# Moving two groups of an expert's rows into a scheduled list, and giving routing rows a buffer each

## The chip, the cores and the metric

The kernel runs on one core of one Trainium2 chip. The metric is the device time of one execution in microseconds (us), the median of the runs shown. A core has TensorE (PE, matrix products), VectorE (DVE), ScalarE (ACT) and GpSimd (POOL) for the work, and SyncE (SP), which here issues nearly all DMA transfers. Each engine takes its instructions in the order in which the program gives them to it.

## What is computed

Three layers follow each other: a gated delta attention, a mixture of experts in which every token goes through all 8 experts (weights from 8 Sinkhorn rounds), and a second mixture in which each token goes to its one best expert.

```
# attention, per batch and head, 768 steps, head_dim 48
y[t]  = q[t] @ state
state = state + beta[t] * outer(k_n[t], v[t] - k_n[t] @ state)
# first mixture: x is (3072, 384), w1 (8, 384, 1024), w2 (8, 1024, 384)
P = exp(x @ w_gate - max);  8 times: P /= P.sum(1); P /= P.sum(0); P *= N / E
out = sum over e of P[:, e] * (relu(x @ w1[e]) @ w2[e])
# second mixture: cosine logits / tau, argmax, one expert per token
out[mask_e] = gate_w[mask_e] * (relu(x[mask_e] @ w1[e]) @ w2[e])
```

## The kernel before

Tokens lie in 24 tiles of 128, which make 6 groups of 512. Matrix products run in float16 with a high and a low half for each operand, so each product is three matmuls.

**The attention's list.** The attention, the whole of expert 0, and the first half of expert 1's hidden units (4 of 8 blocks of 128) are nodes of a list. A small planner, class `Sched`, walks through the nodes with a table of costs (`HOP` from one engine to another, a cost for each node, and a choice of engines where a node has several) and so sets the order in which each engine gets its instructions; it runs while the program is built. The expert nodes (line 824 for the first layer, 848 for the second) fill TensorE between attention nodes. Their results for each tile are copied by ScalarE (858) and stored by SyncE to DRAM: `y0d` for expert 0, `y1d` for expert 1's first half (859). The Sinkhorn rounds are nodes of the same list. At its end stand the first layer of group 0 of expert 1's second half (1050) and the second layer of tile 0 (1063). In the list a second-layer result `py` has one PSUM buffer (pool `ps2`).

**Behind the list** everything is written in loops. SyncE loads the accumulator `accb` (24 tiles, 4.7 MB) from `y0d` in six transfers (1197). `moe1_group(1, W, g)` loads the group's four tiles of `y1d` (374), runs the first layer (352, with ScalarE 335 and VectorE 336 splitting each block of 512 into halves), and then, tile by tile, the second layer (363); for expert 1 each tile then gets ScalarE's scaling of `accb` by expert 0's weight (383), VectorE's adding of the `y1d` half (384) and of `py` (387). Here `py` has two buffers (`ps3`), as has the first layer's `pt`. Between the steps `run` calls `bg()`, every third step, which puts a piece of the next expert's weight preparation into the program (`prep_w`: load into `st` 286 and 288, six maxima 295, a maximum over partitions by GpSimd 302, six splits by ScalarE 274 and VectorE 275, and so twice for each expert).

**The routing.** Expert 7 of the first mixture and the routing of the second are a second list. For each group of four tiles the best expert and a place in a table are worked out; `row` (token number and weight) is written by GpSimd into the table with four indirect transfers (1446), at the places in `ri`. `row` has two buffers, so the copy that begins the row of group g (1420) waits until the transfers of group g - 2 have landed.

Of the kernel before, what the change touches and what calls it, by code (L numbers as in the profile page):

```python
# [165 lines left out]
def kernel(  # L166
# [202 lines left out]
    def moe1_group(e, W, g):  # L369

        fs, x = (FH, "b") if e == 1 else (0, e)
        if e == 1:
            yh_ = st2.tile([128, 4, DM], F32, name="yh", tag="yh", bufs=2)
            nc.sync.dma_start(out=yh_, in_=y1d[4 * g:4 * g + 4].rearrange("t p d -> p t d"))
        if (e, g) != (1, 0):
            yield from mlp1(W, xh[g], xl[g], 512, hh, hl, fs)
# [41 lines left out]
    with (  # L418
# [623 lines left out]
        o1 = {}  # L1042
        pn = None
        for f_ in range(FH):
            for kk in range(KD):
                def f(slot=None, f_=f_, kk=kk):
                    if kk == 0:
                        o1[f_] = ps1.tile([128, 512], F32, name="pt")
                    for x, (wv, xv) in enumerate(((0, xh), (0, xl), (1, xh))):
                        nc.tensor.matmul(out=o1[f_], lhsT=w1v(W1, wv, kk, FH + f_), rhs=xv[0][:, kk], start=kk == 0 and x == 0, stop=kk == KD - 1 and x == 2)  # L1050
                Q((f"h{f_}_{kk}", "e1"), "P", 648, f, [pn] if pn else [("xb", 0), mend] + w1a, 2e6,
                  ps=("pt", 1) if kk == 0 else None, cols=1536, moe=True)
                pn = (f"h{f_}_{kk}", "e1")
            wr = [mend]
            Q((f"rl{f_}", "e1"), "A", 478, lambda f_=f_: nc.scalar.activation(out=hh[f_], in_=o1[f_], func=AF.Relu), [pn] + wr, NT - 1.0)
            Q((f"rs{f_}", "e1"), "V", 602, lambda f_=f_: nc.vector.scalar_tensor_tensor(
                out=hl[f_], in0=o1[f_], scalar=0.0, in1=hh[f_], op0=ALU.max, op1=ALU.subtract), [(f"rl{f_}", "e1")], NT - 1.0, frees=(f"h{f_}_0", "e1"))
        for f_ in range(FH):
            def f(slot=None, f_=f_):
                if f_ == 0:  # L1060
                    pye.append(ps2.tile([128, 512], F32, name="py"))
                for x, (a_, b_) in enumerate(((hh, 0), (hh, 1), (hl, 0))):
                    nc.tensor.matmul(out=pye[0][:, 0:DM], lhsT=a_[f_][:, 0:128], rhs=w2v(W1, b_, FH + f_),
                                     start=(f_ == 0 and x == 0), stop=(f_ == FH - 1 and x == 2))
            Q((f"g{f_}", "e1"), "P", 488, f, [pn, (f"rs{f_}", "e1")] + w1, 2e6, ps=("py", 1) if f_ == 0 else None, cols=1152, moe=True)
            pn = (f"g{f_}", "e1")
# [231 lines left out]
    def route_tile(g, j):  # L1298
# [72 lines left out]
    def route_group(g):  # L1371
# [350 lines left out]
```

## Time and profile before

| | us |
|---|---|
| median of 3 runs | 2196.34 (2196.14 to 2198.1) |
| the profiled execution, its own time | 2194.12 |
| its span, first to last instruction | 2192.3 |
| PE busy | 2046.6 (93%) |
| DVE busy | 1227.4 (56%) |
| ACT busy | 849.9 (39%) |

The profile gives for each engine the time in which it works, and for its idle time what ended it. TensorE is busy nearly all the time, so what counts is where it isn't, and what it waits for there. Matmuls overlap in its pipeline; the distance of the starts tells the true cost. The list of the attention ends for TensorE at about 702 us, expert 1 at 798 us, expert 6 at about 1738 us; the second mixture begins at about 1960 us.

### The profile page before, as it was taken

Reading aid. Unit: us, or ns where it says so; the run is one execution under the profiler, and the core shown is the slowest. Engines: PE = TensorE matmul, PEld = TensorE weight load, DVE = VectorE, ACT = ScalarE, POOL = GpSimd, SP = SyncE. Lnnn points to the kernel's source line nnn. Section 1 sums busy time; section 2 is a strip of 40 time slices with the busy share of each in tenths; the row PEclk is TensorE's granted clock in tenths of the full one; section 3 lists DMA queues with packets and bytes.
Section 4 is the critical chain, followed back from the end, with each engine's and each line's share of the span. In section 5 each row is a group of like instructions: output and inputs, shape, how many; then the busy total and the mean of one; then the engine's idle time right before and its main releaser. Section 6 shows DMA issues by size and latency. Waiting matters only on the chain. (4 is left out here: it accounts for less than half of the span.)

```text
span 2192.3 us, 46083 instructions
## 1 busy us (share of the span) xinstructions
PE 2046.6 (93%) x19340; PEld 1293.5 (59%) x19340; DVE 1227.4 (56%) x2815; ACT 849.9 (39%) x1600; POOL 277.3 (13%) x322
## 2 busy tenths in 40 slices
PE   2688999999998999999999999999999989999999
PEld 2667777777765445555555555555555545557777
DVE  7988888888771665445445545554552245552111
ACT  5766756566532332223222322222221134352332
POOL 5322323233100000000000000000000000112221
PEclk9799999999999999999999999999999999999999
DMA  2546666566534220231132123113220001049765
GB/s 88 111 98 117 130 118 113 106 124 119 129 97 148 71 85 29 87 114 59 58 116 87 59 87 107 67 58 116 76 69 1 1 19 26 19 136 345 273 238 204
DMA packets 367237, 224.90 MB, mean 103 GB/s; under 512 B 301916, under 2 KB 346880, under 8 KB 360626
## 3 DMA queue, kind: packets, MB, share of 16 engines
q1 hardware_dynamic: 362738, 211.66, 34.7%
q0 software_dynamic: 4288, 10.25, 1.4%
q8 instruction: 153, 2.51, 0.5%
q14 instruction: 58, 0.48, 0.1%
HBM read 138.28 MB, written 50.36 MB: 86 GB/s over the span
## 5 line engine op out<-in xcount | busy, mean ns | idle before, releaser
L352 PE MATMUL pt<-big,W 128*128 128x512 f16 x2340 | 512.6, 379 | 3.5 <-DVE hhl L336 2.0
L352 PEld LDWEIGHTS <-W 128*128 128x128 f16 x2340 | 229.0, 98 | 277.5 <-issue 6.8
L363 PE MATMUL py<-W,hhl 128*128 128x384 f16 x1716 | 302.1, 327 | 9.0 <-DVE accb L387 9.0
L335 ACT ACTIVATE hhl<-pt 128x512 f16<-128x512 f32 x140 | 83.5, 596 | 520.5 <-PE pt L352 514.8
L363 PE MATMUL py<-W,ttb 128*128 128x384 f16 x1440 | 253.6, 326 | 0.0
L363 PEld LDWEIGHTS <-hhl 128*128 128x128 f16 x1716 | 168.4, 98 | 125.5 <-issue 11.8
L387 DVE SCALAR_TENSOR_TENSOR accb<-py,pet,accb 128x384 f32<-128x384 f32 x144 | 88.8, 617 | 198.4 <-PE py L363 196.5
L363 PEld LDWEIGHTS <-ttb 128*128 128x128 f16 x1440 | 140.9, 98 | 93.1
L824 PE MATMUL pt<-xring,W 128*128 128x256 f16 x1296 | 185.3, 278 | 4.5 <-ACT xring L482 2.4
L336 DVE SCALAR_TENSOR_TENSOR hhl<-pt,hhl 128x512 f16<-128x512 f32 x140 | 96.7, 691 | 149.8 <-ACT hhl L335 149.8
L848 PE MATMUL py<-W,hhl 128*128 128x384 f16 x864 | 171.2, 327 | 4.9 <-ACT yo L858 3.2
L336 DVE SCALAR_TENSOR_TENSOR ttb<-pt,ttb 128x512 f16<-128x512 f32 x120 | 82.8, 690 | 92.7 <-ACT ttb L335 92.6
L295 DVE TENSOR_REDUCE wmx<-st 128x1 f32<-128x512 f32 x168 | 110.3, 677 | 39.7 <-DMA st<-in_moe_w_dram 39.7
L302 POOL PARTITION_ALL_REDUCE wma<-wm x28 | 10.4, 370 | 965.1 <-DVE wm L300 965.1
L824 PEld LDWEIGHTS <-W 128*128 128x128 f16 x1296 | 114.3, 100 | 19.6 <-issue 4.6
L335 ACT ACTIVATE ttb<-pt 128x512 f16<-128x512 f32 x120 | 71.5, 595 | 136.7 <-PE pt L352 136.0
L1251 PEld LDWEIGHTS <-W 128*128 128x128 f16 x1008 | 90.6, 98 | 57.2 <-issue 7.2
L1271 PE MATMUL py<-W,hhl 128*128 128x384 f16 x624 | 110.8, 330 | 0.0
L1251 PE MATMUL pt<-big,W 128*128 128x512 f16 x432 | 98.5, 379 | 5.4 <-DVE hhl L1257 5.4
L848 PEld LDWEIGHTS <-hhl 128*128 128x128 f16 x864 | 73.4, 98 | 44.0 <-issue 4.5
L1257 DVE SCALAR_TENSOR_TENSOR ttb<-pt,ttb 128x512 f16<-128x512 f32 x50 | 34.6, 691 | 109.8 <-ACT ttb L1256 99.8
L478 DVE TENSOR_TENSOR Z<-pz,cs 128x512 f16<-128x512 f32 x120 | 80.4, 675 | 12.3 <-PE pz L464 11.8
(359 smaller groups left out, 3094.4 us busy)
## 6 DMA issues: line engine op xcount, KB each, us to landing
st<-in_moe_w_dram SPq DMA_DIRECT2D x28, 1536.0 KB, 10.0
W<-w2d SPq DMA_DIRECT2D x18, 1536.0 KB, 7.7
w2d<-big SPq DMA_DIRECT2D x16, 1536.0 KB
big<-w2d SPq DMA_DIRECT2D x8, 1536.0 KB, 12.3
accb<-w2d SPq DMA_DIRECT2D x8, 1536.0 KB, 7.7
big<-kqc SPq DMA_DIRECT2D x90, 128.0 KB, 4.0
KQ<-in_kq_dram SPq DMA_DIRECT2D x23, 384.0 KB, 4.1
big<-KQ SPq DMA_DIRECT2D x84, 96.0 KB, 3.6
```

What stands on the lines that cost most here:

```text
L295: nc.vector.tensor_reduce(out=mx[:, c:c + 1], in_=st[:, c * CW:c * CW + CW], op=ALU.max, axis=AX.X, apply_absolute_value=True)
L335: nc.scalar.activation(out=oh, in_=pt, func=AF.Relu)
L336: nc.vector.scalar_tensor_tensor(out=ol, in0=pt, scalar=0.0, in1=oh, op0=ALU.max, op1=ALU.subtract)
L352: nc.tensor.matmul(out=po, lhsT=lhsT, rhs=rhs, start=(i == 0), stop=(i == 3 * KD - 1))
L363: nc.tensor.matmul(out=py[:, 0:DM], lhsT=lhsT, rhs=rhs, start=(n == 0), stop=(n == 3 * (KF - fs) - 1))
L387: nc.vector.scalar_tensor_tensor(out=acc[t], in0=py[:, 0:DM], scalar=pe[x][:, t:t + 1], in1=acc[t], op0=ALU.mult, op1=ALU.add)
L478: ENG[e].tensor_tensor(out=out, in0=in0, in1=in1, op=op)
L824: nc.tensor.matmul(out=o[g4][:, 256 * j:256 * j + 256], lhsT=w1v(W, wv, kk, f_), rhs=XR[:, xv, kk], start=(kk == 0 and x == 0), stop=(kk = ...
L848: nc.tensor.matmul(out=o["py"][:, 0:DM], lhsT=a_[f_ // per][:, c_:c_ + 128], rhs=w2v(W, b_, f_), start=(f_ == 0 and x == 0), stop=(f_ == n ...
L1251: nc.tensor.matmul(out=po, lhsT=w1v(W, wv, kk, f), rhs=xv[:, kk, :], start=(kk == 0 and x == 0), stop=(kk == KD - 1 and x == 2))
L1257: V((f"rs{q_}", id_), lambda q_=q_: nc.vector.scalar_tensor_tensor(out=HL[q_], in0=o[q_], scalar=0.0, in1=HH[q_], op0=ALU.max, op1=ALU.sub ...
L1271: nc.tensor.matmul(out=o["py"][:, 0:DM], lhsT=a_[f // per][:, c_:c_ + 128], rhs=w2v(W, b_, f), start=(f == 0 and x == 0), stop=(f == KF - ...
```

## The change

Five edits go together.

- Groups 0 and 1 of expert 1's second half (`GW = 2`) become nodes at the end of the attention's list, with both layers. Their eight results are copied by ScalarE and stored to a new DRAM array `y2d`. Behind the list only groups 2 to 5 run through `moe1_group`; the eight tiles of groups 0 and 1 are put together by a new generator, `woven_group`, which `bg()` steps in between: it loads `y1d` and `y2d` of a tile, and three steps later ScalarE scales `accb` and VectorE adds the two.
- The background is stepped at every second step, no longer at every third, while expert 1 runs.
- Loads are reordered: the first half of expert 2's weights is loaded ahead of `accb`; `y1d` comes two tiles at a time, in two buffers.
- The planner's table: a DMA's hop 3000 for 2200, and other costs for some VectorE and GpSimd nodes.
- `row` and `ri` of the routing get a buffer for each group, and three nodes no longer name the table's transfer of group g - 2.

```diff
-    HOP = {"P": 200.0, "V": 135.0, "A": 150.0, "G": 100.0, "D": 2200.0}
+    HOP = {"P": 200.0, "V": 135.0, "A": 150.0, "G": 100.0, "D": 3000.0}
...
-        if e == 1:
-            yh_ = st2.tile([128, 4, DM], F32, name="yh", tag="yh", bufs=2)
-            nc.sync.dma_start(out=yh_, in_=y1d[4 * g:4 * g + 4].rearrange("t p d -> p t d"))
-        if (e, g) != (1, 0):
-            yield from mlp1(W, xh[g], xl[g], 512, hh, hl, fs)
+        if e == 1 and g == GW:
+            y1_load(4 * g)
+            y1_load(4 * g + 2)
+        yield from mlp1(W, xh[g], xl[g], 512, hh, hl, fs)
...
                 if py is not None:
                     if e == 1:
-                        nc.scalar.activation(out=acc[t], in_=acc[t], func=AF.Copy, scale=pe[0][:, t:t + 1])
-                        nc.vector.scalar_tensor_tensor(
-                            out=acc[t], in0=yh_[:, j], scalar=pe[1][:, t:t + 1], in1=acc[t], op0=ALU.mult, op1=ALU.add
-                        )
+                        first_acc(t, y1s[t // 2][:, j % 2])
+                        if j % 2 and t + 4 < NT:
+                            y1_load(t + 3)
...
+    def woven_group(g):
+        for t in range(4 * g, 4 * g + 4):
+            yg = st2.tile([128, DM], F32, name="yg", bufs=2)
+            nc.sync.dma_start(out=yg, in_=y1d[t])
+            yz = st2.tile([128, DM], F32, name="yz", bufs=2)
+            nc.sync.dma_start(out=yz, in_=y2d[t])
+            yield 1
+            yield 1
+            yield 1
+            first_acc(t, yg)
+            nc.vector.scalar_tensor_tensor(
+                out=acc[t], in0=yz, scalar=pe["b"][:, t:t + 1], in1=acc[t], op0=ALU.mult, op1=ALU.add
+            )
+            yield 1
...
-        VG4 = (("V", 470), ("G", 872))
+        VG4 = (("V", 500), ("G", 915))
+        VGP = (("V", 1050), ("G", 1235))
...
-            N("ptl", VG5, 0, lambda e: ttt(e, o["PTc"][:, 1], o["PT"], o["PTc"][:, 0], ALU.subtract), ["pth"])
+            N("ptl", VGP, 0, lambda e: ttt(e, o["PTc"][:, 1], o["PT"], o["PTc"][:, 0], ALU.subtract), ["pth"])
...
+                def f(t_=t_, g=g, o1=o1):
+                    ob = hp.tile([128, DM], F32, name="yo")
+                    nc.scalar.copy(out=ob, in_=o1["py"][:, 0:DM])
+                    nc.sync.dma_start(out=y2d[4 * g + t_], in_=ob)
+                Q((f"yo{t_}", e1), "A", 413, f, [pn], NT - 1.0, frees=(f"g{t_}_0", e1))
...
-    queue(prepq, iter([1] * 10))
-    queue(prepq, prep1(2))
+    first_prep = prep1(2)
+    next(first_prep)
+    queue(prepq, iter([1] * 4), first_prep)
...
-        for g in range(NG):
-            run(moe1_group(e, W, g))
+        if e == 1:
+            queue([], iter([1] * 4), *(woven_group(g) for g in range(GW)))
+        for g in range(GW if e == 1 else 0, NG):
+            run(moe1_group(e, W, g), 2 if e == 1 else 3)
...
-            o["row"] = s2.tile([128, T, 2], I32, name="row")
+            o["row"] = s2.tile([128, T, 2], I32, name="row", bufs=NG)
```

The node `ml` (the low half of a matrix M) goes from 602 to 1000 on VectorE and from 1115 to 1605 on GpSimd; `first_acc` holds the two instructions that stood in the loop, and `y1_load(t)` loads tiles t and t + 1.

What stands where on SyncE, at the end of the list: before, the stores of `y1d` (859), then the six loads of `accb` (1197), then `yh`.

```order
L859 DMA y1d<-yo 128x384 x4
L1197 DMA accb<-y0d 128x4x384 x6
L374 DMA yh<-y1d 128x4x384 x2
L286 DMA st<-in_moe_w_dram 128x3x1024
L374 DMA yh<-y1d 128x4x384 x2
```

In the change, at the same place:

```order
L1100 DMA y2d<-yo 128x384 x8
L287 DMA st<-in_moe_w_dram 128x3x1024
L1233 DMA accb<-y0d 128x4x384 x6
L395 DMA yh<-y1d 128x2x384 x2
L404 DMA yg<-y1d 128x384
L406 DMA yz<-y2d 128x384
```

The eight stores of `y2d`, which come as the eight tiles are done, and the weight load now stand ahead of `accb`.

VectorE at the first tiles that are put together behind the list (`yh` and `yg` are halves from `y1d`, `yz` is from `y2d`, `wmx<-st` a maximum of the weight preparation). Before, tiles 0 to 2:

```order
L384 SCALAR_TENSOR_TENSOR accb<-yh,pet,accb 128x384
L387 SCALAR_TENSOR_TENSOR accb<-py,pet,accb 128x384
L384 SCALAR_TENSOR_TENSOR accb<-yh,pet,accb 128x384
L387 SCALAR_TENSOR_TENSOR accb<-py,pet,accb 128x384
L384 SCALAR_TENSOR_TENSOR accb<-yh,pet,accb 128x384
L387 SCALAR_TENSOR_TENSOR accb<-py,pet,accb 128x384
```

In the change, tile 8, woven tile 0, and tiles 9 and 10:

```order
L399 SCALAR_TENSOR_TENSOR accb<-yh,pet,accb 128x384
L386 SCALAR_TENSOR_TENSOR accb<-py,pet,accb 128x384
L296 TENSOR_REDUCE wmx<-st 128x1
L399 SCALAR_TENSOR_TENSOR accb<-yg,pet,accb 128x384
L411 SCALAR_TENSOR_TENSOR accb<-yz,pet,accb 128x384
L296 TENSOR_REDUCE wmx<-st 128x1
L399 SCALAR_TENSOR_TENSOR accb<-yh,pet,accb 128x384
L386 SCALAR_TENSOR_TENSOR accb<-py,pet,accb 128x384
L296 TENSOR_REDUCE wmx<-st 128x1 x2
L399 SCALAR_TENSOR_TENSOR accb<-yh,pet,accb 128x384
L386 SCALAR_TENSOR_TENSOR accb<-py,pet,accb 128x384
```

Between two tiles of the main loop there now stand a woven tile, maxima, or both.

VectorE in the routing, end of the first group and first layer of the third (1257 and 1295 are the second half of a first-layer split, `qri` and `ri` the places). Before:

```order
L1440 TENSOR_REDUCE qrr<-qrk 128x4
L1257 SCALAR_TENSOR_TENSOR hhl<-pt,hhl 128x512
L1441 CAST qri<-qrr 128x4
L1257 SCALAR_TENSOR_TENSOR ttb<-pt,ttb 128x512 x3
L1420 COPY row<-toki 128x4
L1257 SCALAR_TENSOR_TENSOR ttb<-pt,ttb 128x512
```

In the change:

```order
L1478 TENSOR_REDUCE qrr<-qrk 128x4
L1295 SCALAR_TENSOR_TENSOR hhl<-pt,hhl 128x512
L1481 CAST ri<-qrr 128x4
L1295 SCALAR_TENSOR_TENSOR ttb<-pt,ttb 128x512 x4
L1503 SCALAR_TENSOR_TENSOR accb<-py,pet,accb 128x384
```

The copy of `row` is gone from here; all six stand at the beginning of this list.

## Rows read from the trace of the kernel before

**Rows 1.** Windows: busy time and count of each engine, granted clock, DMA.

```profile
core 0: us, PE busy (x) PEld busy (x) DVE busy (x) ACT busy (x) POOL busy (x), PEclk, DMA share, GB/s
200.00:640.00 440.00, 410.65 (x7728) 325.39 (x7723) 361.24 (x862) 269.57 (x568) 115.03 (x111) 1.00 0.61 121
...
714.30:798.00 83.70, 82.78 (x433) 42.97 (x433) 54.57 (x100) 29.34 (x52) 1.68 (x4) 0.98 0.25 82
```

**Rows 2.** Timeline of PE around the list's end: start, us, instruction, idle before.

```profile
682.91 4.09 PE L824 MATMUL pt<-xring,W 128*128 128x256 f16 x36
...
689.85 2.11 PE L848 MATMUL py<-W,hhl 128*128 128x384 f16 x12 [0.61 <-ACT yo L858]
691.80 7.93 PE L1050 MATMUL pt<-big,W 128*128 128x512 f16 x36
699.57 2.11 PE L1063 MATMUL py<-W,hhl 128*128 128x384 f16 x12
701.52 4.06 PE L363 MATMUL py<-W,hhl 128*128 128x384 f16 x24
714.30 4.00 PE L363 MATMUL py<-W,hhl 128*128 128x384 f16 x12 [8.71 <-DVE accb L387]
...
797.82 9.88 PE L352 MATMUL pt<-big,W 128*128 128x512 f16 x45
```

**Rows 3.** Timeline of SP, the same stretch.

```profile
680.94 11.93 SPq L859 DMA_DIRECT2D y1d<-yo  x4
693.04 5.43 SPq L1197 DMA_DIRECT2D accb<-y0d  x6
```

**Rows 4.** Timeline of DVE behind the list.

```profile
711.65 0.62 DVE L384 SCALAR_TENSOR_TENSOR accb<-yh,pet,accb 128x384 f32<-128x384 f32 x1 [10.55 <-DMA yh<-y1d]
...
756.25 0.68 DVE L336 SCALAR_TENSOR_TENSOR hhl<-pt,hhl 128x512 f16<-128x512 f32 x1
756.86 0.74 DVE L275 SCALAR_TENSOR_TENSOR W<-st,w0s,W 128x512 f16<-128x512 f32 x1
...
759.17 1.42 DVE L275 SCALAR_TENSOR_TENSOR W<-st,w0s,W 128x512 f16<-128x512 f32 x2
760.50 0.61 DVE L384 SCALAR_TENSOR_TENSOR accb<-yh,pet,accb 128x384 f32<-128x384 f32 x1
...
761.75 0.74 DVE L275 SCALAR_TENSOR_TENSOR W<-st,w0s,W 128x512 f16<-128x512 f32 x1
...
774.99 1.27 DVE L295 TENSOR_REDUCE wmx<-st 128x1 f32<-128x512 f32 x2
776.18 0.61 DVE L384 SCALAR_TENSOR_TENSOR accb<-yh,pet,accb 128x384 f32<-128x384 f32 x1
```

**Rows 5.** Tile st, 690 to 900 us: its loads, from issue to landing.

```profile
DMA to landing us min/median/max: 6.8/10.1/13.5
```

**Rows 6.** Windows in and after TensorE's long wait.

```profile
705.60:708.00 2.40, 0.00 (x0) 0.00 (x0) 0.00 (x0) 0.00 (x0) 0.00 (x0) 1.00 1.07 374
708.00:718.00 10.00, 3.70 (x12) 1.77 (x12) 4.05 (x7) 0.00 (x0) 0.00 (x0) 0.50 0.85 300
```

**Rows 7.** Timelines of DVE and PE in the routing.

```profile
1798.63 0.17 DVE L1420 COPY row<-toki 128x4 int32<-128x4 int32 x1 [10.05 <-DMA tab<-row,qri]
...
1799.45 0.50 PE L1271 MATMUL py<-W,ttb 128*128 128x384 f16 x1 [6.54 <-DVE ttb L1257]
1799.75 4.05 PE L1271 MATMUL py<-W,hhl 128*128 128x384 f16 x12
...
1839.08 0.34 PE L1271 MATMUL py<-W,ttb 128*128 128x384 f16 x1 [1.76 <-DVE ttb L1257]
```

**Rows 8.** Waits of PE from 200 to 640 us: total, times, longest.

```profile
PE pg L635 <- DMA big<-kqc: 4.8, 3, 2.3
PE pz L618 <- DMA big<-KQ: 3.7, 5, 1.2
```

**Rows 9.** Line 478: PTc (node ptl) on DVE, ns min/median/max.

```profile
L478 DVE TENSOR_TENSOR PTc<-PT,PTc x14: 639/1276/1762, 68.1 to 511.5; 128x512 f16<-128x512 f32 x14
```

More of the change, by code (lines that the diff above doesn't have):

```diff
@@ L28 @@
 NA = 3
+GW = 2
 NF = 11
@@ L199 @@
     y1d = DR.tile([NT, 128, DM], F32, name="y1d")
+    y2d = DR.tile([4 * GW, 128, DM], F32, name="y2d")
     tab = DR.tile([TROWS, 2], I32, name="tab")
@@ L379, in moe1_group @@
             sl = slice(128 * j, 128 * j + 128)
-            for py in pye[:1] if (e, t) == (1, 0) else mlp2(W, lambda f: hh[f][:, sl], lambda f: hl[f][:, sl], fs):
+            for py in mlp2(W, lambda f: hh[f][:, sl], lambda f: hl[f][:, sl], fs):
                 if py is not None:
                     if e == 1:
-                        nc.scalar.activation(out=acc[t], in_=acc[t], func=AF.Copy, scale=pe[0][:, t:t + 1])
-                        nc.vector.scalar_tensor_tensor(
-                            out=acc[t], in0=yh_[:, j], scalar=pe[1][:, t:t + 1], in1=acc[t], op0=ALU.mult, op1=ALU.add
-                        )
+                        first_acc(t, y1s[t // 2][:, j % 2])
+                        if j % 2 and t + 4 < NT:
+                            y1_load(t + 3)
                     nc.vector.scalar_tensor_tensor(
@@ L390, in moe1_group, with y1_load, first_acc @@
                 yield 1
+    y1s = {}
+    def y1_load(t):
+        y1s[t // 2] = st2.tile([128, 2, DM], F32, name="yh", bufs=2)
+        nc.sync.dma_start(out=y1s[t // 2], in_=y1d[t:t + 2].rearrange("t p d -> p t d"))
+    def first_acc(t, yh_):
+        nc.scalar.activation(out=acc[t], in_=acc[t], func=AF.Copy, scale=pe[0][:, t:t + 1])
+        nc.vector.scalar_tensor_tensor(out=acc[t], in0=yh_, scalar=pe[1][:, t:t + 1], in1=acc[t], op0=ALU.mult, op1=ALU.add)
+    def woven_group(g):
[12 more added lines that the diff above has]
+            yield 1
     def bc(ap, n=8):
@@ L1040 @@
             Q(("xb", g), "D", 1300, f, bigdeps(g) + [("x1", 4 * g + 1), ("x1", 4 * g + 3)], NT + 1.0 + g, lat=1500.0)
[L1042 to L1066, printed above, removed]
+        pn = mend
@@ new lines, with f @@
+        for g in range(GW):
+            e1 = f"e1{g}"
+            o1 = {}
+            wr = pn
+            for f_ in range(FH):
+                for kk in range(KD):
+                    def f(slot=None, f_=f_, kk=kk, g=g, o1=o1):
+                        if kk == 0:
+                            o1[f_] = ps1.tile([128, 512], F32, name="pt")
+                        for x, (wv, xv) in enumerate(((0, xh), (0, xl), (1, xh))):
+                            nc.tensor.matmul(out=o1[f_], lhsT=w1v(W1, wv, kk, FH + f_), rhs=xv[g][:, kk], start=kk == 0 and x == 0, stop=kk == KD - 1 and x == 2)
+                    Q((f"h{f_}_{kk}", e1), "P", 648, f, [pn] if f_ or kk else [pn, ("xb", g)] + w1a, 2e6 + g,
+                      ps=("pt", 1) if kk == 0 else None, cols=1536, moe=True)
+                    pn = (f"h{f_}_{kk}", e1)
+                Q((f"rl{f_}", e1), "A", 478, lambda f_=f_, o1=o1: nc.scalar.activation(out=hh[f_], in_=o1[f_], func=AF.Relu), [pn, wr], NT - 1.0)
+                Q((f"rs{f_}", e1), "V", 602, lambda f_=f_, o1=o1: nc.vector.scalar_tensor_tensor(
+                    out=hl[f_], in0=o1[f_], scalar=0.0, in1=hh[f_], op0=ALU.max, op1=ALU.subtract), [(f"rl{f_}", e1)], NT - 1.0, frees=(f"h{f_}_0", e1))
+            for t_ in range(4):
+                for f_ in range(FH):
+                    def f(slot=None, f_=f_, t_=t_, o1=o1):
+                        if f_ == 0:
+                            o1["py"] = ps2.tile([128, 512], F32, name="py")
+                        for x, (a_, b_) in enumerate(((hh, 0), (hh, 1), (hl, 0))):
+                            nc.tensor.matmul(out=o1["py"][:, 0:DM], lhsT=a_[f_][:, 128 * t_:128 * t_ + 128], rhs=w2v(W1, b_, FH + f_),
+                                             start=(f_ == 0 and x == 0), stop=(f_ == FH - 1 and x == 2))
+                    Q((f"g{t_}_{f_}", e1), "P", 488, f, [pn, (f"rs{f_}", e1)] + w1, 2e6 + g, ps=("py", 1) if f_ == 0 else None, cols=1152, moe=True)
+                    pn = (f"g{t_}_{f_}", e1)
+                def f(t_=t_, g=g, o1=o1):
[3 more added lines that the diff above has]
+                Q((f"yo{t_}", e1), "A", 413, f, [pn], NT - 1.0, frees=(f"g{t_}_0", e1))
@@ L1312, in f @@
             nc.scalar.activation(out=junk, in_=acc[t], func=AF.Square, accum_out=R()[1][:, j:j + 1])
-        node2(("sn", id_), "A", 520, f, [("acc", t), ("sc", g - 2)], prio=pr)
+        node2(("sn", id_), "A", 520, f, [("acc", t), ("rw", g - 2)], prio=pr)
         def f():
@@ L1392, in route_group @@
         sns = [("sn", 4 * g + j) for j in range(T)]
-        q("m", lambda: vt.tensor_reduce(out=tl("m", [T]), in_=R()[0], op=ALU.max, axis=AX.X), lgs + [("sc", g - 2)], cost=100)
+        q("m", lambda: vt.tensor_reduce(out=tl("m", [T]), in_=R()[0], op=ALU.max, axis=AX.X), lgs + [("ri", g - 2), ("rw", g - 2)], cost=100)
         q("l2", lambda: vt.tensor_tensor(out=tl("l2", [T, E]), in0=R()[0], in1=b3(o["m"]), op=ALU.subtract), ["m"], cost=100)
@@ L1399, in route_group @@
         q("oh", lambda: vt.tensor_tensor(out=tl("oh", [T, E], F16), in0=b2_(eio), in1=b3(o["fi"]), op=ALU.is_equal), ["fi"], cost=100)
-        q("s1", lambda: vt.tensor_scalar(out=R()[1], in0=R()[1], scalar1=1e-36, scalar2=None, op0=ALU.max), sns + [("sc", g - 2)])
+        q("s1", lambda: vt.tensor_scalar(out=R()[1], in0=R()[1], scalar1=1e-36, scalar2=None, op0=ALU.max), sns + [("rw", g - 2)])
         q("s0", lambda: nc.scalar.activation(out=tl("sr", [T]), in_=R()[1], func=AF.Ln), ["s1"], "A", 220)
@@ L1440, in route_group, with f @@
         q("rr", lambda: vt.tensor_reduce(out=tl("rr", [T]), in_=o["rk"], op=ALU.add, axis=AX.X), ["rm"], cost=100)
-        q("ri", lambda: vt.tensor_copy(out=tl("ri", [T], I32), in_=o["rr"]), ["rr"])
+        def f():
+            o["ri"] = s2.tile([128, T], I32, name="ri", bufs=NG)
+            vt.tensor_copy(out=o["ri"], in_=o["rr"])
+        q("ri", f, ["rr"])
         def f():
```

5 lines of the change are left out of this document (2 added, 3 removed).

## The prediction

> **What bounds the kernel now.** I read the windows by stage first, then the waits, then timelines of the places where TensorE stands still. TensorE is busy 93% of the span, so an edit counts only where it isn't. In the middle of the attention's list it is idle for 29 of 440 us, while VectorE is busy 82% of that stretch [rows 1]. At the end of the list the reader should see this sequence: SyncE waits for the last stores of `y1d` and only then, at 693.04, issues the `accb` loads [rows 3]; the `yh` tile queued behind them is there at 711.65, 18.6 us later, and releases VectorE [rows 4]; TensorE, having gone two tiles ahead, stands for 8.71 us [rows 2]. The clock then is half, and the next tile's 12 matmuls take 3.8 us to the next start instead of 1.95 [rows 2, 6]. In the routing VectorE stands for 10.05 us before a copy of 0.17 us into `row`, because the table's transfers of two groups earlier have not landed; behind it in VectorE's queue waits the split that TensorE needs [rows 7].
>
> **The change part by part.** The profiled execution took 2194.12 us (span 2192.3, 1.8 around it); the median of the runs is 2.2 us higher. The sum is made against 2194.1 and moved by 2.2 at the end.
>
> *Routing rows.* The order shows the six copies of `row` ahead of the whole list, so nothing on VectorE waits for the table any more. TensorE gets back 6.54 and 1.76 us of waiting and the slow tile between (4.05 against 2.11 us: 1.9) [rows 2, 7]: -10.2 us. The other two waits of this kind didn't reach TensorE. The transfers themselves stay on GpSimd, in the same order, and the second mixture's lookups follow them at the same distance. Bounds: -8.3 if the clock falls there for another reason, -10.7 if the small waits around it go too. I take -10.2.
>
> *Two groups into the list.* TensorE's work is the same, elsewhere. Call the moment when expert 1's second half begins T0, 691.80 before; expert 2 began at 797.82, so the six groups took 106.0 us [rows 2]. A first layer is 7.77 us (691.80 to 699.57) and a tile of the second layer 1.95, so a group is 15.6 and six are 93.4; the other 12.6 are the wait, the slow tile and small things.
>
> Now the steps in the change. (a) Both groups in the list: 31.1 us. There `py` has one buffer, and each tile that follows another waits for ScalarE's copy, as at 689.85 (0.61) [rows 2]: six such places, 3.7 us. T0 + 34.8. (b) What becomes of the loads? In SyncE's order the eight stores of `y2d` stand ahead of `accb`, so the loads can't be issued before the last tile is copied. Before, they were issued 1.2 us after TensorE had left the list's last store tile (691.80 to 693.04) [rows 2, 3]; the two groups that might have covered them are over. T0 + 36.0. (c) How long they take: before, 4.7 MB and 0.8 MB of `yh` in 18.6 us. Now 1.57 MB of expert 2's weights stand ahead and the first `yh` is 0.4 MB: 1.2 MB more, at 374 GB/s [rows 6] 3.2 us. VectorE has tile 8's `yh` at T0 + 57.8. TensorE meanwhile does group 2's first layer and two tiles, 11.7 us from T0 + 34.8, and then both `py` buffers are full: it stands from T0 + 46.5 to T0 + 59.2, 12.7 us where it was 8.7, and pays the slow tile again (1.8).
>
> [...]
>
> (d) What is queued on VectorE behind that wait. The order has, from tile 8 to tile 19: 20 pairs of accumulations (12 tiles, 8 woven ones), 12 maxima, 12 weight splits, 8 first-layer splits. Spaced start to start these cost 1.25 a pair (760.50 to 761.75), 0.60 (774.99 to 776.18, two), 0.665 (759.17 to 760.50, two) and 0.61 [rows 4]: 25.0 + 7.1 + 8.0 + 4.9 = 45.0 us. To this come 1.9 us in which VectorE waits for the second half of the weights (that load can start only when `st` is free, takes 6.8 us [rows 5], and has four pairs, 5.0 us, ahead of it), and an estimated 4 for small instructions and for handing over. VectorE so ends with tile 19 about 51 to 52 us after it began. TensorE needs for tiles 10 to 19 only 10 x 1.95 + 2 x 7.77 us, with its start 1.4 us after VectorE's and the slow tile 38. It can't run ahead: two `pt` and two `py` buffers. So it follows VectorE and finishes tile 19 about 50.2 us after the wait's end; group 5 adds 15.6. Expert 2 begins at T0 + 57.8 + 65.8 = T0 + 123.6, against 106.0: **+17.6**. Before, the same stretch had VectorE busy for 54.6 of 83.7 us [rows 1], with 5 groups to spread the preparation over; now the preparation, the woven tiles and stepping at every second step fall together. Bounds: +6 if VectorE keeps up after all (only the 12.7, the slow tile and the 3.7 count), +21 if TensorE's clock falls in two of the later waits too (1.8 each).
>
> *The list's table.* This only reorders. The waits of TensorE for the two big transfers within the list are 8.5 us from 200 to 640 us [rows 8], and a longer hop puts expert work ahead of what waits for them. By the order, 276 first-layer and 192 second-layer expert matmuls followed the last attention matmul before; now 252 and 171 do, at 4.09 / 36 and 1.95 / 12 us 6.2 us less to do at the end [rows 2]. If attention ends when it did, T0 comes 6 us sooner. But VectorE's share doesn't shrink: `PTc` falls from 14 to 11 there, while casts of `t` rise from 4 to 11 and `tt` from 7 to 10, some 2 us more. Bounds: -12 (all of those waits and some of the others among the 29 us) and +6 (the same by bad luck the other way). Nearest is the shift in the order less VectorE's share: **-4**.
>
> Sum: 2194.1 - 10.2 + 17.6 - 4 = 2197.5, as a median 2199.7: 3.4 us over before, 0.15%. About 0.2% (4.4 us) is what a measurement can tell from no change.
>
> **The rivals.** *The list gains nothing* (decided on the slower side). Its durations, such as 1276 ns for `PTc`, are no property of the node: the same instruction took 639 at best and 1762 at worst [rows 9], depending on what else ran. A new order has other neighbours, so the numbers may fit no better, and VectorE's extra 2 to 3 us move T0 to later. Price: 2194.1 - 10.2 + 17.6 + 3 = 2204.5, as a median 2206.7. It decides from T0 staying above about 691. The Trainium skill, SBUF — State Buffer, section SBUF: two separate sides, names such a cause: VectorE with two inputs from SBUF and GpSimd lock each other out of a shared port for a whole instruction. The spread of the rows agrees with it.
>
> *VectorE keeps up behind the list.* The background then fits between the tiles, as before the change, where TensorE lost no more than some 0.3 us at a time there. For it: the small waits of the old trace. Against it: 45 us of work in 38. Price: +6 in place of +17.6, 2188.1 as a median. It decides from VectorE's instructions standing much closer than now.
>
> *The list gains much.* T0 12 us sooner: 2191.7. For it, idle time in the list; against it, that most of it waits for VectorE and ScalarE, not for DMA.
>
> *The routing wait only moves*, to another reader of the table: 2199.7 + 10.2 = 2209.9. The order shows no such reader.
>
> **How the numbers follow.** Forecast 0.37, list gains nothing 0.25, VectorE keeps up 0.20, list gains much 0.13, wait moves 0.05. The likeliest one's own range is 2195 to 2204. With the others the range is 2188 to 2209, which leaves out the rest of the fourth case's tail and the last. Faster by over 0.2%: most of the third and half of the fourth, 0.25. Within: half of the first, parts of those two, 0.32. Slower: nearly all of the second, the fifth, and 0.13 of the first's upper half, 0.43.
>
> **What would show it.** Right: SyncE's `accb` loads begin after the last `y2d` store; TensorE stands some 12 to 13 us about 12 us later, before tile 10; VectorE is busy over 85% for the next 45 us, with TensorE waiting for `pt` and `py` several times for 1 to 4 us; expert 2 begins 121 to 127 us after T0; T0 lies at 685 to 691; groups of the routing follow each other at one distance. Wrong: loads issued earlier, a wait below 10 us, T0 above 693 or below 682.

## The result: 13 us slower

| | median us | runs |
|---|---|---|
| before | 2197.11 | 6 (2194.05 to 2198.32) |
| after | 2210.35 | 6 (2204.54 to 2215.76) |

The ratio is 1.0065 [1.0053, 1.0077], 13.2 us more. The forecast was 2199.7 in a range of 2188 to 2209: too low, with the result 1.35 us above the range. The profiled execution of after took 2206.33 us, 4.0 under its median.

**Around the list's end.** TensorE's timeline answers to [rows 2]. The two groups are lines 1079 and 1092, groups 2 to 5 lines 353 and 364, and 818.58 is the start of expert 2.

```profile
687.65 7.93 PE L1079 MATMUL pt<-big,W 128*128 128x512 f16 x36
...
698.15 2.11 PE L1092 MATMUL py<-W,hhl 128*128 128x384 f16 x12 [0.61 <-ACT yo L1099]
...
723.62 2.11 PE L1092 MATMUL py<-W,hhl 128*128 128x384 f16 x12 [2.76 <-ACT yo L1099]
725.57 7.93 PE L353 MATMUL pt<-big,W 128*128 128x512 f16 x36
...
748.53 6.17 PE L364 MATMUL py<-W,hhl 128*128 128x384 f16 x24 [11.13 <-DVE accb L386]
...
781.43 4.04 PE L353 MATMUL pt<-big,W 128*128 128x512 f16 x18 [3.28 <-DVE hhl L337]
...
790.97 2.11 PE L364 MATMUL py<-W,hhl 128*128 128x384 f16 x12 [1.60 <-DVE accb L386]
...
796.67 5.99 PE L353 MATMUL pt<-big,W 128*128 128x512 f16 x27
804.58 0.81 PE L353 MATMUL pt<-big,W 128*128 128x512 f16 x3 [1.91 <-DVE ess L1124]
807.74 0.49 PE L1177 MATMUL pen<-cs,ench 8*128 8x8 f32 x3 [2.35 <-DVE ench L1172]
...
818.58 6.64 PE L353 MATMUL pt<-big,W 128*128 128x512 f16 x30
```

T0 is 687.65, 4.15 us sooner than before. Expert 2 begins at T0 + 130.9, where it was T0 + 106.0. Tile 19 is done at 796.67; the last group then takes 21.9 us, with two waits at instructions of the second mixture's setup (`ess`, `ench`).

SyncE's timeline answers to [rows 3], VectorE's and ScalarE's to [rows 4].

```profile
698.12 28.51 SPq L1100 DMA_DIRECT2D y2d<-yo  x8
726.73 0.39 SPq L287 DMA_DIRECT2D st<-in_moe_w_dram  x1
727.22 8.07 SPq L1233 DMA_DIRECT2D accb<-y0d  x6
735.33 3.83 SPq L395 DMA_DIRECT2D yh<-y1d  x2
```

```profile
747.13 0.62 DVE L399 SCALAR_TENSOR_TENSOR accb<-yh,pet,accb 128x384 f32<-128x384 f32 x1 [12.27 <-DMA yh<-y1d]
...
802.60 0.16 DVE L1165 RECIPROCAL itau<-tau 128x1 f32<-128x1 f32 x1 [2.40 <-DMA tau<-in_moe_tau_dram]
```

```profile
718.22 0.48 ACT L1099 COPY yo<-py 128x384 f32<-128x384 f32 x1 [2.24 <-PE py L1092]
723.09 0.48 ACT L1099 COPY yo<-py 128x384 f32<-128x384 f32 x1 [4.39 <-DMA y2d<-yo]
```

The loads of `accb` go out after the last store of `y2d`, and VectorE gets the first `yh` 19.9 us after the first of them. The second copy shows a wait that the forecast did not have: `yo` has one buffer, and its store was not yet through.

VectorE's load behind that wait, in a window up to its last instruction for tile 19, answers to [rows 1].

```profile
core 0: us, PE busy (x) PEld busy (x) DVE busy (x) ACT busy (x) POOL busy (x), PEclk, DMA share, GB/s
...
747.13:798.58 51.45, 40.01 (x201) 20.28 (x201) 44.86 (x85) 19.17 (x34) 1.46 (x4) 0.94 0.44 144
```

VectorE is busy 87% of it, TensorE 78%.

**The routing and what follows it.** GpSimd's timeline: 1487 writes a group's rows into the table (the first of four transfers is shown), 1615 gathers rows of `x2d` for the second mixture.

```profile
1800.27 1.31 POOL L1487 DMA_INDIRECT tab<-row,ri  x1 [172.16 <-DVE ri L1481]
...
1942.68 0.96 POOL L1487 DMA_INDIRECT tab<-row,ri  x1 [30.78 <-DVE mA L1536]
...
1963.45 0.95 POOL L1615 DMA_INDIRECT xg<-x2d,tb  x1 [0.30 <-issue]
1970.50 0.94 POOL L1615 DMA_INDIRECT xg<-x2d,tb  x1 [6.11 <-DMA x2d<-xr]
...
2004.82 0.98 POOL L1615 DMA_INDIRECT xg<-x2d,tb  x1 [9.42 <-DMA tb<-tab]
```

The same places before the change:

```profile
1783.16 1.31 POOL L1446 DMA_INDIRECT tab<-row,qri  x1 [147.71 <-DVE qri L1441]
...
1936.30 0.95 POOL L1446 DMA_INDIRECT tab<-row,qri  x1 [30.78 <-DVE mA L1495]
...
1956.74 0.95 POOL L1574 DMA_INDIRECT xg<-x2d,tb  x1 [0.30 <-issue]
1957.99 0.95 POOL L1574 DMA_INDIRECT xg<-x2d,tb  x1 [0.30 <-issue]
...
1994.47 0.98 POOL L1574 DMA_INDIRECT xg<-x2d,tb  x1 [9.59 <-DMA tb<-tab]
```

From the first to the fifth group it took 153.1 us and now takes 142.4: 10.7 less, and VectorE's waits of [rows 7] are gone. From the fifth group to the third round of gathers it took 58.2 and now takes 62.1. There the fourth gather, which went out 1.25 us after the third, waits 6.11 us for a store of `x2d`.

So the span's 12.3 us (2204.6 against 2192.3) come from five places: T0 -4.15, expert 1 +24.9, experts 2 to 6 -3.7 (936.4 us from 818.58 to the first matmul of expert 7 at 1754.97, before 940.0), expert 7 with the routing -10.7 (187.7 us for 198.4), and +5.9 from the fifth group to the end (261.9 for 256.0).

### The profile page after: what moved, and what is told of

Read it like the earlier page. It is cut to its first block, busy times and chain, and to the rows that moved or that the text cites. A ratio compares the mean times of both kernels' runs of the same rounds, so it can differ in the third digit from the quotient of the medians.

```text
span 2204.6 us, 46116 instructions
## 1 busy us (share of the span) xinstructions
PE 2048.1 (93%) x19340; PEld 1294.4 (59%) x19340; DVE 1237.6 (56%) x2821; ACT 851.8 (39%) x1600; POOL 278.9 (13%) x324
## 4 chain that ended last, share of the span: by engine, by line
PE 60%; DMA 4%; DVE 4%; ACT 2%; issue 1%; SPq 1%; POOL 0%; ACTq 0%; POOLq 0%; DVEq 0%
PE pt L353 20%; PE py L364 20%; PE py L1309 8%; PE pt L1289 7%; DMA st<-in_moe_w_dram 2%; PE pt L849 1%; PE py L873 1%; DMA xg<-x2d,tb 1%; PE pt L1079 1%; PE py L1092 1%; DMA yh<-y1d 1%; DVE wmx L296 0%; SPq L1233 0%; PE px L1623 0%; ACT L1441 0%
## 5 line engine op out<-in xcount | busy, mean ns | idle before, releaser
L353 PE MATMUL pt<-big,W 128*128 128x512 f16 x2304 | 505.4, 380 | 8.5 <-DVE hhl L337 6.6
L364 PE MATMUL py<-W,hhl 128*128 128x384 f16 x1632 | 288.3, 328 | 16.0 <-DVE accb L386 15.9
L364 PEld LDWEIGHTS <-hhl 128*128 128x128 f16 x1632 | 160.4, 98 | 128.0 <-issue 20.2
L386 DVE SCALAR_TENSOR_TENSOR accb<-py,pet,accb 128x384 f32<-128x384 f32 x136 | 83.9, 617 | 184.0 <-PE py L364 182.2
L849 PE MATMUL pt<-xring,W 128*128 128x256 f16 x1296 | 180.6, 275 | 3.6 <-DVE hhl L862 3.6
L873 PE MATMUL py<-W,hhl 128*128 128x384 f16 x864 | 175.0, 328 | 5.3 <-ACT yo L883 4.6
L337 DVE SCALAR_TENSOR_TENSOR hhl<-pt,hhl 128x512 f16<-128x512 f32 x136 | 93.9, 691 | 151.8 <-ACT hhl L336 151.8
L849 PEld LDWEIGHTS <-W 128*128 128x128 f16 x1296 | 113.3, 98 | 17.5 <-DVE hhl L862 2.0
L1309 PE MATMUL py<-W,hhl 128*128 128x384 f16 x624 | 108.9, 326 | 0.0
L1289 PE MATMUL pt<-big,W 128*128 128x512 f16 x432 | 98.5, 379 | 5.4 <-DVE hhl L1295 5.4
L873 PEld LDWEIGHTS <-hhl 128*128 128x128 f16 x864 | 73.1, 99 | 42.9 <-issue 7.7
L1295 DVE SCALAR_TENSOR_TENSOR hhl<-pt,hhl 128x512 f16<-128x512 f32 x52 | 35.8, 688 | 96.1 <-ACT hhl L1294 90.0
```

What stands on the lines that cost most here:

```text
L337: nc.vector.scalar_tensor_tensor(out=ol, in0=pt, scalar=0.0, in1=oh, op0=ALU.max, op1=ALU.subtract)
L364: nc.tensor.matmul(out=py[:, 0:DM], lhsT=lhsT, rhs=rhs, start=(n == 0), stop=(n == 3 * (KF - fs) - 1))
L386: nc.vector.scalar_tensor_tensor(out=acc[t], in0=py[:, 0:DM], scalar=pe[x][:, t:t + 1], in1=acc[t], op0=ALU.mult, op1=ALU.add)
L849: nc.tensor.matmul(out=o[g4][:, 256 * j:256 * j + 256], lhsT=w1v(W, wv, kk, f_), rhs=XR[:, xv, kk], start=(kk == 0 and x == 0), stop=(kk = ...
L873: nc.tensor.matmul(out=o["py"][:, 0:DM], lhsT=a_[f_ // per][:, c_:c_ + 128], rhs=w2v(W, b_, f_), start=(f_ == 0 and x == 0), stop=(f_ == n ...
L1289: nc.tensor.matmul(out=po, lhsT=w1v(W, wv, kk, f), rhs=xv[:, kk, :], start=(kk == 0 and x == 0), stop=(kk == KD - 1 and x == 2))
```

## The experiments

All medians stand beside runs of the kernel before on the same chip, at 2192.6 to 2195.1 us in the four sets.

| run | median us | minus before | ratio |
|---|---|---|---|
| routing_alone | 2185.08 | -9.6 | 0.9946 [0.9928, 0.9964] |
| table_first_list | 2191.49 | -3.2 | 0.9983 [0.9974, 0.9992] |
| groups_alone | 2216.26 | +21.6 | 1.0098 [1.0080, 1.0117] |
| second_list_2200 | 2203.67 | +9.0 | 1.0033 [1.0022, 1.0044] |
| hop_3000_second_list | 2199.05 | +4.0 | 1.0016 [1.0007, 1.0025] |
| setup2_later | 2198.81 | +4.0 | 1.0016 [1.0006, 1.0027] |
| no_woven_adds | 2196.81 | +2.0 | 1.0004 [0.9993, 1.0014] |
| loads_first | 2183.03 | -11.8 | 0.9937 [0.9924, 0.9950] |
| routing_and_table | 2182.20 | -12.6 | 0.9945 [0.9932, 0.9958] |
| loads_first_late | 2180.48 | -14.6 | 0.9934 [0.9914, 0.9954] |
| loads_first_prep | 2181.97 | -13.1 | 0.9939 [0.9921, 0.9956] |
| loads_first_prep_34 | 2173.96 | -18.6 | 0.9915 [0.9902, 0.9929] |

### The parts alone

**routing_alone** is the routing edit by itself on the kernel before: a buffer for each group in `row` and `ri`. Three nodes wait for the row and the places of group g - 2 in place of the table's transfers, and the copy that begins `row` waits for nothing.

> The kernel before with the routing edit alone (a place in row and ri for each group, three nodes that no longer name the table's transfer of two groups earlier). Theory: TensorE's two waits of 6.54 and 1.76 us and the slow tile go and nothing takes their place, so about 10.5 us less than before (-9 to -11.5), with the groups of the routing 35.6 us apart from the first to the last. Rival 1: part of the gain is lost behind the routing, because the edit also changes the order of the gathers and stores of x2d; then only 4 to 6 us less. Rival 2: the wait goes to another reader of the table; within 2 us of before.

-9.6 us, and the five groups are 35.6 us apart throughout (1783.08, 1818.65, 1854.27, 1889.88, 1925.49 in its trace). The theory holds; no other reader of the table took over the wait.

**table_first_list**: hop and node costs, with the second list left as it was.

```diff
+    HOP = {"P": 200.0, "V": 135.0, "A": 150.0, "G": 100.0, "D": 3000.0}
...
     sch = Sched({"pt": 2, "py": 2, "m": 3})
+    sch.HOP = dict(Sched.HOP, D=2200.0)
```

> The kernel before with the planner's table alone (hop of a DMA 3000, new costs for four kinds of nodes), and only in the attention's list: the list of the routing keeps 2200. Theory: the 4.15 us by which expert 1's second half began sooner in the changed kernel come from the table, so -3 to -5 us. Rival: they come from the two groups that stand in the list in the changed kernel and give the planner more to fill with; then the table alone is worth -1 to +6 us.

**groups_alone**: the two groups, the woven tiles, the loads and the background, without table and routing.

> The kernel before with the two groups in the list, the woven tiles, the reordered loads and the denser background, but with the old table and the old routing. Theory: expert 1's second half takes about 25 us longer and experts 2 to 6 give some 4 us back, so +19 to +23 us over before. Rival: what was lost in expert 1 is partly the new table's or the routing's doing, so that the groups alone cost +12 to +17 us, close to the forecast's term.

The first matmul of expert 1's second half, on TensorE's timeline of table_first_list, and then of groups_alone:

```profile
689.77 3.40 PE L1051 MATMUL pt<-big,W 128*128 128x512 f16 x15
```

```profile
689.30 4.05 PE L1078 MATMUL pt<-big,W 128*128 128x512 f16 x18
```

And of routing_and_table (below), which has the same attention list as table_first_list:

```profile
686.54 7.93 PE L1051 MATMUL pt<-big,W 128*128 128x512 f16 x36
```

Against 691.80 [rows 2] T0 is 2.0 us sooner with the table in one trace and 5.3 sooner in another, though the list is the same; with the groups alone it is 2.5 sooner in the one trace there is. So single traces can't divide the 4.15 us between the table and the groups. As a median the table alone gives 3.2 us, within the theory's 3 to 5. The groups as a whole cost 21.6 us, as their theory said (+19 to +23).

**second_list_2200** is the changed kernel with the line `sch.HOP = ...` above in the second list, **hop_3000_second_list** the kernel before with 3000 only there.

> The changed kernel, with the DMA hop back at 2200 in the list of expert 7 and the routing alone; the attention's list keeps 3000. In that second list the longer hop puts the first store of x2d between the third and the fourth gather of the second mixture; here all four gathers stand ahead of it again, as in the kernel before. Theory: the 5.9 us that were lost between the last group of the routing and the end come from that order, so -5 to -7 us against the changed kernel (about 8 us over the kernel before). Rival: they come from where the routing now ends or from the clock; within 2 us of the changed kernel.

> The kernel before with nothing changed but the DMA hop in the list of expert 7 and the routing: 3000 for 2200. The fourth gather of the second mixture then stands behind a store of x2d. Theory: this order costs what second_list_2200 gave back, +3 to +7 us over before, and the trace has GpSimd waiting some 6 us for that store. Rival: the loss needs the routing edit as well (the groups end sooner); within 2 us of before.

GpSimd in hop_3000_second_list, the third and fourth gather and the third round, and then SyncE's stores of `x2d`:

```profile
1954.39 0.95 POOL L1575 DMA_INDIRECT xg<-x2d,tb  x1 [0.30 <-issue]
1961.34 0.94 POOL L1575 DMA_INDIRECT xg<-x2d,tb  x1 [6.00 <-issue]
...
1996.34 0.98 POOL L1575 DMA_INDIRECT xg<-x2d,tb  x1 [11.01 <-DMA tb<-tab]
```

```profile
1957.85 9.85 SPq L1339 DMA_DIRECT2D x2d<-xr  x6
```

And the fourth gather in second_list_2200:

```profile
1967.17 0.95 POOL L1616 DMA_INDIRECT xg<-x2d,tb  x1 [0.30 <-issue]
```

The hop alone makes the fourth gather wait and costs 4.0 us; put back, the wait goes and 4 to 7 us return (the medians' distance to before falls from 13.2 to 9.0, the ratio by 0.0032). It needs no routing edit. The row of the 6.00 us names no releaser; that it is the store of `x2d` follows from the order, and from the changed kernel's row, which names it. From the fifth group to the end the two traces with 3000 in this list take 261.9 and 263.5 us, the twelve with 2200 between 254.7 and 258.9, with the routing edit or without. So of the +5.9 us there the hop is shown for some 4, and the rest lies within what traces differ by.

The four parts add up, as far as their intervals tell: -9.6 - 3.2 + 21.6 + 4.0 = +12.8, for 13.2 measured.

### What the groups lose

**loads_first** writes the two groups out behind the list, with the loads ahead of their stores on SyncE; its base is second_list_2200, as that of the next two.

```diff
-        for g in range(GW):
-            e1 = f"e1{g}"
...
+    def early_group(g):
+        yield from mlp1(W1, xh[g], xl[g], 512, hh, hl, FH)
+        for t in range(4 * g, 4 * g + 4):
+            sl = slice(128 * (t % 4), 128 * (t % 4) + 128)
+            for py in mlp2(W1, lambda f: hh[f][:, sl], lambda f: hl[f][:, sl], FH):
+                if py is not None:
+                    ob = st2.tile([128, DM], F32, name=("yg", "yz")[t % 2], bufs=2)
+                    nc.scalar.copy(out=ob, in_=py[:, 0:DM])
+                    nc.sync.dma_start(out=y2d[t], in_=ob)
+                yield 1
+
+    y1_load(4 * GW)
+    y1_load(4 * GW + 2)
+    for g in range(GW):
+        drain(early_group(g))
```

> Base: the changed kernel with the hop of 2200 in the second list (second_list_2200). Here the two groups are taken out of the list and written out by hand right behind it, the same instructions in the same order on TensorE, but with the loads of st, accb and the first yh ahead of the stores of y2d on SyncE, two py buffers, and the tiles yg and yz as the buffers from which y2d is stored. Theory: the 11.1 us for which TensorE stands in expert 1 come from the order on SyncE alone, so they go, with the slow tiles behind them (2.1) and the waits for the one py buffer (5.8 in all): expert 2 begins 111 to 115 us after the list's end (130.9 in the changed kernel), and the time falls by 16 to 19 us against the base. Rival 1: VectorE's work sets the length of expert 1 whenever the loads come; then less than 8 us. Rival 2: the stores now wait behind 6 MB of loads, and TensorE waits for their buffers instead; also less than 8 us, with waits of TensorE for ScalarE's copies.

SyncE and then TensorE in loads_first:

```profile
689.74 9.40 SPq L1196 DMA_DIRECT2D accb<-y0d  x6
699.18 3.83 SPq L392 DMA_DIRECT2D yh<-y1d  x2
703.11 0.95 SPq L1206 DMA_DIRECT2D y2d<-yg  x1
```

```profile
688.09 7.93 PE L353 MATMUL pt<-big,W 128*128 128x512 f16 x36
...
762.67 4.04 PE L353 MATMUL pt<-big,W 128*128 128x512 f16 x18 [3.21 <-DVE hhl L337]
...
801.34 15.70 PE L353 MATMUL pt<-big,W 128*128 128x512 f16 x72
```

The loads leave 1.65 us after the list's last expert tile, TensorE never stands for them, and expert 1's second half is 113.3 us. By the medians' distances to before it is 20.8 us less than the base, a little more than the theory's 16 to 19. So the long wait and the slow list came from the groups' place in the list, with their stores ahead of the loads on SyncE and with the one `py` and the one `yo`. The run changes these together; in the changed kernel's trace the stand behind the loads and the slow tiles cost 13.2 us, the waits for `py` and `yo` 6.8. The shorter waits from VectorE, such as 3.21, stay: 10.9 us in all, where the changed kernel has 10.0.

**setup2_later**:

```diff
-    queue(prepq, setup2())
+    queue(prepq, iter([1] * 14), setup2())
```

> Base: second_list_2200. The background queue gets 14 empty steps ahead of setup2 (norms of the second mixture's expert vectors), so that it falls into expert 2 as in the kernel before, and no longer into the last group of expert 1. Theory: group 5 of expert 1 took 21.9 us in the changed kernel where a group's matmuls take 15.6, because SyncE's loads for setup2 are issued late and VectorE stands before them with the first-layer splits queued behind; without it 16 to 17 us, and setup2 costs some 1.5 us in expert 2: 3 to 5 us less than the base. Rival: the slack is used by the next thing in the background, or expert 2 waits for it; within 2 us of the base.

Its last group of expert 1, on TensorE's timeline (812.71 is expert 2):

```profile
797.14 7.93 PE L353 MATMUL pt<-big,W 128*128 128x512 f16 x36
...
812.71 9.88 PE L353 MATMUL pt<-big,W 128*128 128x512 f16 x45
```

15.6 us, where the changed kernel has 21.9 and the base's own trace 23.3. As a median it is 3.7 (by the ratios) to 5.0 us less (by the distances to before). The theory holds for group 5. But `setup2` costs 3.8 us in expert 2 and not 1.5, as the first transfer into the table shows:

```profile
1798.05 1.31 POOL L1488 DMA_INDIRECT tab<-row,ri  x1 [147.71 <-DVE ri L1482]
```

From expert 2's beginning to it this is 985.3 us, as in the kernel before (797.82 to 1783.16) and in loads_first_late and loads_first_prep_34, which also have `setup2` in expert 2. With `setup2` in expert 1 it is 981.7 us in the changed kernel (818.58 to 1800.27) and 981.5 in loads_first. So the gain of the changed kernel in experts 2 to 6 is `setup2`, which had moved out of them.

**no_woven_adds** drops the two additions of `woven_group`.

> Base: second_list_2200. The woven tiles (0 to 7) leave out their 16 additions on VectorE (the halves of y1d and y2d are loaded and not added); ScalarE's scaling stays. Theory: behind the long wait VectorE's work of some 45 us sets the pace, so that 16 additions of 0.62 us, 10 us less for it, leave TensorE's own 38 us as the limit: 7 to 10 us less than the base, and the waits of TensorE for hhl and accb between tile 10 and group 5 go. Rival: TensorE's waits there come from loads and ScalarE; less than 3 us.

TensorE, and the windows' row for the stretch from the end of VectorE's wait to the end of tile 19:

```profile
778.97 4.04 PE L353 MATMUL pt<-big,W 128*128 128x512 f16 x18 [1.90 <-DVE hhl L337]
...
788.51 2.11 PE L364 MATMUL py<-W,hhl 128*128 128x384 f16 x12 [1.60 <-DVE accb L386]
```

```profile
748.30:793.00 44.70, 38.14 (x192) 19.43 (x192) 34.12 (x66) 19.18 (x34) 1.15 (x4) 0.93 0.46 149
```

7.0 us less by the distances to before, 6.4 by the ratios, about the lower edge of the theory's 7 to 10; but the theory's place for them holds only in part. The stretch shrinks by 4.8 us, from 49.5 (747.13 to 796.67) to 44.7, while VectorE is busy for only 34 of them, and TensorE's waits in it fall from 10.0 to 5.2 us and don't go. So VectorE's amount of work explains about half. The waits that stay (1.90 and 1.60, the latter as in the changed kernel) come from what stands ahead in its queue and waits itself, such as a maximum that waits 2.72 us for its load of `st`.

### Versions that keep the gains

**routing_and_table** leaves expert 1 as it was.

> The kernel before with the routing edit and with the table in the attention's list only; expert 1 as before. Theory: the two gains add up, about 10 us and 3 to 4 us, so 12 to 15 us less than before. Rival: they share a part (the end of the list and the routing are far apart, so no mechanism is known); 8 to 11 us less.

-12.6 us, near the sum of the two parts (-9.6 and -3.2).

**loads_first_late** adds the 14 steps to loads_first; **loads_first_prep** instead also steps the background in the two groups; **loads_first_prep_34** changes its 32 empty steps to 34.

```diff
-    queue(prepq, iter([1] * 4), first_prep)
-    queue(prepq, setup2())
+    queue(prepq, iter([1] * 2), first_prep)
+    queue(prepq, iter([1] * 32), setup2())
...
-        drain(early_group(g))
+        run(early_group(g))
```

> loads_first, with the 14 empty steps ahead of setup2 as in setup2_later. Theory: the two gains have separate places (the wait behind the list, and group 5), so the 3.7 to 4.9 us of setup2_later come on top: about 16 us less than before, 3 to 5 less than loads_first. Rival: with the wait gone VectorE has slack at the end of expert 1, and setup2 costs nothing there; within 2 us of loads_first.

> loads_first, with the background stepped already while the two groups run (every third step), so that the maxima and splits of the first half of expert 2's weights fall where VectorE has little to do (9 of 53 us), and with setup2 behind expert 1. Theory: TensorE's waits for hhl and accb in groups 3 to 5 (9.7 us and, at setup2, 4.4) come from VectorE's queue, which has preparation, woven tiles and tiles to put together at once; with the preparation done earlier most of them go: 10 to 14 us less than loads_first, some 22 to 26 less than before. Rival: the waits come from the order of the woven tiles within the queue, not from how much stands there; then only the 4 us of setup2 and 1 to 2 more.

> loads_first_prep with 34 empty steps ahead of setup2 in place of 32, so that the maxima of the later experts' weights stand where loads_first_late has them in VectorE's queue. In loads_first_prep expert 1 took 99.6 us, some 10 less than in loads_first_late, but experts 2 and 3 lost 5 us: maxima stood in VectorE's queue 6 to 8 us before their load had landed, and the tiles behind them waited. Theory: that was a matter of where the steps fall, so expert 1 stays at 99 to 101 us and the three waits for accb in experts 2 and 3 go: 4 to 6 us less than loads_first_prep, 17 to 19 less than before. Rival: preparation that is ahead in expert 1 runs into a load that isn't there wherever it stands; the same time as loads_first_prep.

loads_first_late is 2.8 us below loads_first, near the theory's 3 to 5, but the intervals overlap; in its trace expert 1 takes 107.0 us for 113.3, and experts 2 to 6 lose the 3.8 us of `setup2`. In loads_first_prep the theory failed: 10 to 14 us less than loads_first were expected and 1.3 came. Expert 1 did fall to 99.6 us, but from expert 2's beginning to the table it took 10.0 us longer than in loads_first, 3.8 of them for `setup2`. Its VectorE, in experts 2 and 3:

```profile
911.54 1.28 DVE L296 TENSOR_REDUCE wmx<-st 128x1 f32<-128x512 f32 x2 [6.04 <-DMA st<-in_moe_w_dram]
```

```profile
979.04 0.69 DVE L296 TENSOR_REDUCE wmx<-st 128x1 f32<-128x512 f32 x1 [7.97 <-DMA st<-in_moe_w_dram]
979.65 0.61 DVE L383 SCALAR_TENSOR_TENSOR accb<-py,pet,accb 128x384 f32<-128x384 f32 x1
```

A maximum waits for its load and a tile of `accb` waits behind it, for which TensorE stood 4.0 us in three places. TensorE in loads_first_prep_34, with the first matmuls of group 0 and of expert 2:

```profile
684.89 7.93 PE L353 MATMUL pt<-big,W 128*128 128x512 f16 x36
...
784.60 9.88 PE L353 MATMUL pt<-big,W 128*128 128x512 f16 x45
```

Expert 1 again takes 99.7 us, the three waits are gone, and the median is 18.6 us below before, as the theory said (17 to 19): the fastest version, with the two groups early and the routing's and the table's gains kept. Its distance to before is 5.5 us more than loads_first_prep's, though the two intervals overlap a little. Its trace is of its fastest run, 5.2 us under the median, with T0 the earliest of all at 684.89.

## Why the prediction was wrong

- **Routing rows, -10.2**: right. -10.7 in the trace for expert 7 with the routing, -9.6 as a median alone.
- **The table, -4**: right in size for the attention's list, where T0 came 4.15 us sooner and the table alone gives 3.2 as a median (the 6.2 us in its working should be 6.1). "This only reorders" was the first step that failed: the price of reordering was worked out for the attention's list alone, while `HOP` belongs to the class and the list of the routing uses it too. There 3000 put a store of `x2d` ahead of a gather, +4.0 us as a median. No rival had it.
- **(a) T0 + 34.8**: 37.9. Six tiles behind another one cost 0.77 each and not 0.61 (698.15 is 2.73 after its forerunner's start, 1.95 without a wait), and the single `yo` buffer, which was not looked at, 2.15.
- **(b), (c) loads at T0 + 36.0, `yh` at T0 + 57.8**: the first load of `accb` at T0 + 39.6 and `yh` at T0 + 59.5. The mechanism was right. From the first load to `yh` it took 20.4 us (726.73 to 747.13) for the 21.8 forecast, and TensorE stood 11.13 for 12.7.
- **(d) tile 19 done 50.2 us after the wait's end**: 49.5, with VectorE's part ending after 51.45, in the forecast's 51 to 52. The size was right, the reason half right: 10 us of VectorE's work taken away gave 4.8 here.
- **"group 5 adds 15.6"**: the second step that failed, 21.9. With the background stepped oftener, and with 4 empty steps ahead of the preparation for 10 before, `setup2` slid into that group (which of the two moved it was not separated); in it VectorE stands for a load, with the first-layer splits behind. setup2_later shows it. The move also took 3.7 us out of experts 2 to 6, which the forecast left as they were, so its net cost in these traces is 2.6.
- **What was to show it**: T0 at 685 to 691, the loads behind the last store, VectorE over 85% busy, TensorE's short waits, and the groups of the routing at one distance (35.6) came as said; TensorE's stand of 12 to 13 us (11.13) nearly, expert 2 at T0 + 121 to 127 (130.9) not.
- **Sum for the groups, +17.6**: +24.9 at expert 2, made of +3.1 from (a), -1.4 in the following wait, -0.7 in (d), +6.3 in group 5.
- **The rivals**: two have numbers nearer to the measured 2210.35 than the forecast's 2199.7. They are 2206.7 (the list gains nothing) and 2209.9 (the routing wait only moves). That would have been luck: T0 did come sooner, and the routing's waits are gone.

The mechanism of the loss, loads behind the stores of `y2d`, was as foretold. Two effects elsewhere were not followed to their end: the denser background on `setup2`, 2.6 us net, and the hop on the second list, +5.9 in the trace from the fifth group to the end, of which some 4 are shown to be the hop. Between the profiled executions the forecast is 8.8 us short (2206.33 for 2197.5), and these two are 8.5 of it; what else was off nearly cancels. The other 1.8 us of the median's miss (10.65) are that after's median lies 4.0 above its profiled execution, where the forecast added 2.2.

## What to carry to other kernels

A table that a class keeps is used by all its lists: look at the order of every list that it makes, not only at the one that it was changed for. When background work is stepped oftener, ask for each later piece where it now falls, and which loads it waits for while others queue behind it. When work is meant to cover a load, see that its stores don't stand ahead of that load in the queue that carries both: the same two groups cost 21.6 us with their stores ahead of the loads. With the loads ahead, and with more buffers for results and stores, they cost nothing (loads_first at -11.8, routing_and_table without them at -12.6), and a gain of some 6 us came only when the preparation was moved as well (loads_first_prep_34 at -18.6).

## What was not expected of the hardware

**Issuing took longer behind large loads.** On SyncE the two loads of `yh` behind `accb` took 3.83 us to issue, 1.9 each, in the changed kernel and in loads_first. What held them was not tested. One alone, in the changed kernel, took 0.37:

```profile
751.40 0.37 SPq L395 DMA_DIRECT2D yh<-y1d  x1
```

**The clock after one and the same wait.** TensorE's wait in the middle of group 4's first layer was 3.1 to 3.3 us in several kernels. Windows around the 18 matmuls behind it, in loads_first and then in loads_first_late:

```profile
762.60:766.60 4.00, 3.93 (x19) 1.79 (x19) 3.72 (x8) 0.60 (x1) 1.08 (x3) 1.00 0.29 98
```

```profile
761.30:767.20 5.90, 5.81 (x20) 2.36 (x20) 3.83 (x8) 0.64 (x2) 1.07 (x3) 0.71 0.21 69
```

After 3.21 us the granted clock was 1.00 (2.4 GHz); after 3.14 us it was 0.71 as a mean, so that a part of the stretch ran at 1.2 GHz, and the matmuls took 1.7 us longer (5.73 for 4.04). It may be a part of why one kernel's runs differ, by up to 12 us for the kernel before in one set (2191.16 to 2203.21); that wasn't tested.
